# Two groups of the second layer issued by turns, pass for pass, with the product that follows them, in a fused attention and feed-forward kernel

## The chip, the cores and the metric

The kernel runs on one core of a Trainium2 chip. The metric is the device time of one execution in microseconds (us), as the median of several runs. The engines are named as in the profile: PE is the matrix engine, PEld its weight loads, DVE the vector engine, ACT the scalar engine, SP the queue that issues the DMAs.

## The reference

For each of four batches the columns of q and k are normalised over the 6080 tokens, a 256 by 256 score matrix is made and put through a softmax, v is multiplied by it, and the result goes through a feed-forward layer with an exact GELU.

```python
qn = q / (np.linalg.norm(q, axis=1, keepdims=True) + 1e-06)      # q, k, v: (4, 6080, 256)
kn = k / (np.linalg.norm(k, axis=1, keepdims=True) + 1e-06)
s = kn.transpose(0, 2, 1) @ qn / tau
a = np.exp(s - s.max(-1, keepdims=True)); a /= a.sum(-1, keepdims=True) + 1e-09
x = (v @ a).reshape(24320, 256)
h = x @ w_in                                                      # (256, 2048)
g = 0.5 * h * (1.0 + erf(h / sqrt(2)))
out = g @ w_out                                                   # (2048, 256)
```

## The kernel before

**Numbers in two parts.** Every operand of a large product is held as a rounded high part and the rest, the low part. A product of two such operands takes three matmuls into one PSUM bank: high weights by high data, low weights by high data, high weights by low data. They are called the three passes of a group here; `passes` (L649) issues them. Each pass loads its own 128 by 128 weights.

**Steps.** The attention matrix is folded into w_in for each batch (`w_part`, L557), so that the main loop (L1140) is a feed-forward layer over v. It has 4 batches b, 6 pairs p of token tiles in each batch (512 tokens a tile, 480 in the sixth pair) and 8 steps u in each pair, one for two blocks of 128 hidden units: 192 steps. From the third pair of batch 0 on, a step's first layer is seven products instead of eight, by Strassen's scheme (`first_products`, L716, in the order of `ORDER`, L647). They fill two PSUM banks by turns, `one` and `two`: product 0 goes into `one`, product 1 into `two`, product 2 is added onto `one`, product 3 onto `two`, and so on. The two banks are h0 and h1 (both stand as `h` in the profile); which of them is `one` changes from step to step through `ring` (L168 to L177). After product 0 ACT copies bank `one` to SBUF (tile `p`, from `kept`, L721), and product 2 may not touch the bank before that copy is done. After later products DVE adds a kept copy (tile `h`), and ACT makes the GELU of it: as `gh` and `g` with DVE's difference `gl` for two of the four blocks, as `x` for the other two (`whole`, L684), from which `sums` (L691) makes the sums that Strassen's second layer needs.

**The second layer** runs one step behind. `second_products` (L800) is a generator; the main loop takes one group of it after each of the products 0 to 3 of the next step, two after products 4 and 5, and the other three behind the last product (L1149 to L1157, the counts in `PLAN["units"]`). Its first four groups, made by `group` (L819), are 512 (480) columns wide and add gh and gl into the banks c10, c11, c10, c11; these are the large groups. Seven groups of half the width follow, into the banks p0, p1, c00 and c01. So PE's order in a step is product 0, large group 1, product 1, large group 2, product 2, large group 3, product 3, large group 4, product 4, and then products and small groups.

**Work that shares the banks h0 and h1.** At the end of some steps the scores of a later batch are made: `burst` (L286) issues eight matmuls into a bank that it takes from `ring`, and DVE adds that bank onto the tile `sacc`, or copies it there for the first ones of a batch (L295 to L301). In other steps `w_part` issues six matmuls into such a bank, and ACT scales it out into the tile `hl` (with `rden`, L575). Both run from `run(i, 8)`, just ahead of the next step's product 0. The bank that they take is the one that the next step's product 1 writes, because `one` of that step is the other. The steps are set by numbers in `PLAN`: `bursts` and `wpart`, counted from the start of a batch's 48 steps.

**Order.** From step 8 on the three engines' instructions keep the order in which the program issues them (`InOrder`, L179). Semaphore waits are put on the instruction that needs them.

Of the kernel before, what the change touches and what calls it, by code (L numbers as in the profile page):

```python
# [28 lines left out]
NU = NFT // 2  # L29
# [14 lines left out]
PLAN = {  # L44
    "first": {
        "splits": (10, 11, 13, 14, 15, 16, 17, 18, 19, 20, 21, 22, 24, 25, 26, 27, 28, 29, 31, 32, 33, 34),
        "loads": (8, 9, 11, 12, 13, 14, 15, 16, 17, 18, 19, 20, 22, 23, 24, 25, 26, 27, 29, 30, 31, 32),
        "bursts": ((12, 13), (14, 15), (16, 17), (18, 19), (20, 21), (22, 23), (25, 26), (27, 28), (29, 30), (32, 33), (34, 35)),
        "norms": (9, 10, 11, 12, 13, 14, 15, 16, 17, 19, 20, 21, 22, 23, 25, 26, 27, 28, 29, 30, 31, 32, 33, 34),
    },  # L50
    "later": {
        "splits": (2, 3, 5, 6, 7, 8, 10, 11, 13, 14, 16, 17, 19, 20, 21, 22, 24, 26, 27, 28, 30, 32, 33, 34),
# [35 lines left out]
    "halves": 0,  # L88
    "late": 4,
    "wat": 4,  # L90
}

EXTRAS = PLAN["extras"]
# [22 lines left out]
def channel_attention_gelu_ffn(ctx, tc, qk, kqt, vt, tau, w_in, w_out, out):  # L116
# [20 lines left out]
    ps = ctx.enter_context(tc.tile_pool(name="ps", bufs=1, space=bass.MemoryType.PSUM))  # L137

    whs = [const.tile([P, 7, 2, P], F32R, name="wh0")]
    wls = [const.tile([P, 7, 2, P], F32R, name="wl0")]  # L140
# [24 lines left out]
    def psum(name):  # L165
        return ps.tile([P, NT], F32, name=name)
# [3 lines left out]
    def bank():  # L170
        name = ring.popleft()
        ring.append(name)
        return psum(name)
# [21 lines left out]
    mm = pe.matmul  # L195
# [14 lines left out]
    def give(*tiles):  # L210
        for t in tiles:
            room.append(owner.pop(id(t))[0])
# [434 lines left out]
    ORDER = ((A11, B11), (S1, T1), (S2, T2), (S4, B22), (S3, T3), (A12, B21), (A22, T4))  # L647

    def passes(o, wh, wl, hi, lo, start, stop):  # L649
        mm(o, wh, hi, start=start, stop=False, skip_group_check=True)  # L650
        mm(o, wl, hi, start=False, stop=False, skip_group_check=True)
        mm(o, wh, lo, start=False, stop=stop, skip_group_check=True)

    def product(b, p, u, a, v, ps, start, stop):
        n = PAIRS[p][1]
        g, q = divmod(u, 2)
        hi, lo = vops[b, p, v]
        passes(ps[:, :n], whs[g][:, a, q], wls[g][:, a, q], hi[:, :n], lo[:, :n], start, stop)

    def strassen(b, p, u):  # L660
        return (b, p) > (0, 1) and (b, p, u) != (B - 1, NP - 1, NU - 1)
# [3 lines left out]
    def flush():  # L665
        for x in pending:
            x()
        pending.clear()

    def gelu(src, n, i, j):  # L670
        if j == 1:
            gh = pg.tile([P, NT], F32R, name="gh", bufs=2)
            gl = pg.tile([P, NT], F32R, name="gl", bufs=2)
        else:
            gh = pg.tile([P, 4, C] if i == 0 else [P, 3, C], F32R, name=f"gh{i}", bufs=1)
            gl = pg.tile([P, 4, C] if i == 0 else [P, 3, C], F32R, name=f"gl{i}", bufs=1)
            gh, gl = (t.rearrange("p k c -> p (k c)") for t in (gh, gl))
        g = pg.tile([P, NT], F32, name="g", bufs=2)
        act.activation(out=gh[:, :n], in_=src, func=AF.Gelu)
        act.activation(out=g[:, :n], in_=src, func=AF.Gelu)  # L680
        pending.append(lambda: dve.tensor_tensor(out=gl[:, :n], in0=g[:, :n], in1=f32(gh[:, :n]), op=ALU.subtract))
        return gh, gl
# [33 lines left out]
    def first_products(b, p, u):  # L716
# [15 lines left out]
        def do(i, ps, start, stop):  # L732
            product(b, p, u, *ORDER[i], ps, start, stop)
            if u == NU - 1:
                give(*vops.pop((b, p, ORDER[i][1])))
# [34 lines left out]
    def plain_products(b, p, u):  # L770

        n = PAIRS[p][1]
        g, q = divmod(u, 2)
        out = state["blocks"] = {}
        wh, wl = whs[g], wls[g]
        a21 = a21s[g]
        rows = {1: ((wh[:, A11, q], wl[:, A11, q]), (wh[:, A12, q], wl[:, A12, q])),
                0: ((a21[:, 0, q], a21[:, 1, q]), (wh[:, A22, q], wl[:, A22, q]))}
        cols = {0: (B11, B21), 1: (B12, B22)}
        for j in (1, 0):  # L780
            for i in (1, 0):
                ps = bank()
                for k in range(2):
                    hi, lo = vops[b, p, cols[j][k]]
                    passes(ps[:, :n], *rows[i][k], hi[:, :n], lo[:, :n], k == 0, k == 1)
                    if k == 0:
                        yield
                out[i, j] = gelu(ps[:, :n], n, i, j)
                flush()
                if u % 2 == 1 and (i, j) == (0, 0):  # L790
                    give(a21)
                if u == NU - 1 and i == 0:
                    for x in cols[j]:
                        give(*vops.pop((b, p, x)))
                if (i, j) != (0, 0):
                    yield
# [3 lines left out]
    def second_products(b, p, u, blocks):  # L800

        t0, n = PAIRS[p]
        h = n // 2
        wo = wos.pop((b, p, u))
        mine = strassen(b, p, u)
        po = pos.setdefault((b, p), {})
        mixed = any(strassen(b, p, x) for x in range(NU))

        def acc(name):
            first = name not in po  # L810
            if first:
                po[name] = psum(name)
            return po[name], first

        def wpair(c, i):
            cs = slice(c * P, (c + 1) * P)
            return wo[:, 0, i, cs], wo[:, 1, i, cs]

        def group(i, j, c):  # L819
            o, first = acc(f"c{j}{c}")  # L820
            gh, gl = blocks[i, j]
            passes(o[:, :n], *wpair(c, i), gh[:, :n], gl[:, :n], first, u == NU - 1 and i == 0)

        def evict(j, c):
            if c == 0:
                po["osb"] = pg.tile([P, NCT, NT], F32, name="osb", bufs=2)
                act.copy(out=po["osb"][:, 0, :n], in_=po[f"c{j}0"][:, :n])
            else:
                dve.tensor_copy(out=po["osb"][:, 1, :n], in_=po[f"c{j}1"][:, :n])
                store(b, p, j, po["osb"])  # L830

        for i in (1, 0):
            for c in range(NCT):
                group(i, 1, c)
                if u == NU - 1 and i == 0:
                    evict(1, c)
                yield
        if not mine:
            end = u == NU - 1
            for x in range(2 * NCT):  # L840
                c, i = divmod(x, NCT) if end and mixed else (x % NCT, x // NCT)
                i = 1 - i
                group(i, 0, c)
                if end and i == 0:
                    if mixed:
                        merge(b, p, c)
                    else:
                        evict(0, c)
                yield
            return  # L850
        ws = wss.pop((b, p, u))
        (hb, lb), (ht, lt) = blocks["b"], blocks["t"]
        last = not any(strassen(b, p, x) for x in range(u + 1, NU))
        work = (("p0", 0, wpair(0, 1), hb, lb, 0), ("p0", 1, (ws[:, 0, 1], ws[:, 1, 1]), ht, lt, 2),
                ("p1", 0, (ws[:, 0, 0], ws[:, 1, 0]), ht, lt, 0), ("p1", 1, (ws[:, 0, 2], ws[:, 1, 2]), ht, lt, 1),
                ("c00", 1, wpair(0, 0), hb, lb, 2), ("c00", 0, (ws[:, 0, 3], ws[:, 1, 3]), hb, lb, 1),
                ("c01", 1, wpair(1, 0), ht, lt, 3))
        for name, half, w, hi, lo, k in work:
            o, first = acc(name)
            passes(o[:, half * h:(half + 1) * h], *w, hi[:, k * h:(k + 1) * h], lo[:, k * h:(k + 1) * h], first, last)  # L860
            if last and name == "c01" and u < NU - 1:
                flush()
                for _ in combine(b, p):
                    pass
            yield

    def store(b, p, j, osb):

        t0, n = PAIRS[p]
        t = b * N + t0 + j * n  # L870
        dst = out[:, t:t + n].rearrange("(t p) n -> p t n", p=P)
        step = 1 if (b, p) == (B - 1, NP - 1) else NCT
        for c in range(0, NCT, step):
            nc.sync.dma_start(out=dst[:, c:c + step], in_=osb[:, c:c + step, :n])
# [265 lines left out]
    for i, (b, p, u) in enumerate(steps):  # L1140
# [7 lines left out]
        mine = strassen(b, p, u)  # L1148
# [25 lines left out]
        if mine:  # L1174
            next(rest)
        count = 11 if mine else 8
        second = second_products(b, p, u, state.pop("blocks"))
    flush()
    for _ in second:
# [30 lines left out]
```

## Time and profile before

| what | value |
|---|---|
| median of 3 runs (lowest, highest) | 2134.31 us (2133.82, 2134.33) |
| profiled execution, its own time | 2132.88 us |
| its span, first to last instruction | 2131.1 us |
| granted PE clock over the span | 1.000 |
| busy share PE, PEld, DVE, ACT | 100%, 86%, 83%, 77% |
| instructions on PE: matmuls, weight loads | 11255, 11255 |

The timeline view has one row for each instruction: its start in us from the start of the span, its length in us, the engine, the line (L188 is the helper through which all of PE's, DVE's and ACT's work goes), the operation, the tile it writes `<-` the tiles it reads, and the shape. Rows of equal instructions that follow each other are merged (x2). In brackets stands the idle time of that engine ahead of it and who ended it. Matmuls are pipelined: a matmul 512 columns wide has a length of 0.39 us, but the next one starts 0.23 us after it, so that the spacing of starts and not the length is what a matmul costs.

### The profile page before, as it was taken

The page shows a single profiled execution, that of the slowest core. Times are in us where ns is not written, and L with a number is a line of the kernel's source. Part 1 is how long each engine was busy: PE and PEld are TensorE (multiplying, and loading weights), DVE is VectorE, ACT ScalarE, POOL GpSimd, SP SyncE. Part 2 cuts the span into 40 slices and gives each one's busy share as a digit, 9 for nine tenths or more (in the row PEclk, how much of TensorE's full clock was granted, in tenths as well). Part 3 has the DMA queues.
Part 4 walks back from the last instruction along what each step waited for, and adds up shares of the span by engine and source line. Part 5 has one row for each costly group of instructions (what it writes and reads, how often), then busy time and mean ns, then how long its engine had stood idle before and what let it go on. Part 6 is the DMA issues. An engine that isn't in the chain of part 4 may idle for free.

```text
span 2131.1 us, 30717 instructions
## 1 busy us (share of the span) xinstructions
PE 2126.0 (100%) x11255; PEld 1829.4 (86%) x11255; DVE 1764.9 (83%) x2784; ACT 1640.2 (77%) x2708; POOL 1.3 (0%) x8
## 2 busy tenths in 40 slices
PE   9999999999999999999999999999999999999999
PEld 8888888888888888888888888888888888888888
DVE  7987888888888788888888888888888887787786
ACT  6867778868788788776778887877777777777776
POOL 0000000000000000000000000000000000000000
PEclk9999999999999999999999999999999999999999
DMA  9545656554356565544444655554244343343332
GB/s 384 189 162 186 226 186 201 198 183 158 140 176 208 172 204 192 195 166 143 163 159 162 209 179 192 197 196 137 110 167 166 108 151 123 116 155 121 119 133 94
DMA packets 110727, 363.76 MB, mean 171 GB/s; under 512 B 11760, under 2 KB 15984, under 8 KB 108528
## 3 DMA queue, kind: packets, MB, share of 16 engines
q1 hardware_dynamic: 110576, 361.81, 48.8%
q8 instruction: 88, 1.44, 0.3%
q14 instruction: 63, 0.52, 0.1%
HBM read 324.27 MB, written 37.49 MB: 170 GB/s over the span
## 4 chain that ended last, share of the span: by engine, by line
PE 100%; DVE 0%; ACT 0%; issue 0%; DVEq 0%; POOL 0%; POOLq 0%
PE h L188 51%; PE c L188 36%; PE p L188 13%; DVE small L188 0%; DVE t L188 0%; DVE nt L188 0%; ACT t L188 0%; ACT nt L188 0%; DVE diag L188 0%; DVE osb L188 0%; ACT rqs L188 0%; DVEq L1206 0%; ACT small L188 0%; POOL ones L152 0%; POOL ident masks.py:197 0%
## 5 line engine op out<-in xcount | busy, mean ns | idle before, releaser
L188 PE MATMUL h<-v,wh 128*128 128x512 f32 (+1 forms) x2622 | 1026.1, 391 | 0.0
L188 PE MATMUL c<-gh,wo 128*128 128x512 f32 (+3 forms) x2372 | 653.1, 357 | 0.0
L188 PEld LDWEIGHTS h<-v,wh 128*128 128x128 f32 x2622 | 493.9, 188 | 86.1 <-ACT p L188 3.9
L188 PE MATMUL h<-v,wl 128*128 128x512 f32 (+1 forms) x1311 | 513.6, 392 | 0.0
L188 PEld LDWEIGHTS c<-gh,wo 128*128 128x128 f32 x2372 | 433.0, 188 | 83.2
L188 PE MATMUL c<-gl,wo 128*128 128x512 f32 (+3 forms) x1186 | 428.5, 361 | 0.0
L188 DVE TENSOR_TENSOR gl<-x,gh 128x768 fp32r<-128x768 f32 (+1 forms) x350 | 377.0, 1077 | 48.1 <-ACT gh L188 48.0
L188 ACT ACTIVATE gh<-h 128x512 fp32r<-128x512 f32 (+1 forms) x401 | 250.8, 626 | 209.6 <-DVE h L188 195.9
L188 ACT CAST gh<-x 128x768 fp32r<-128x768 f32 (+1 forms) x350 | 327.8, 937 | 31.5 <-DVE x L188 25.1
L188 DVE TENSOR_TENSOR x<-x 128x256 f32<-128x256 f32 (+2 forms) x557 | 274.9, 496 | 57.9 <-ACT x L188 40.0
L188 DVE TENSOR_TENSOR h<-h,p 128x512 f32<-128x512 f32 (+1 forms) x368 | 251.4, 683 | 72.4 <-PE h L188 62.5
L188 DVE TENSOR_TENSOR gl<-g,gh 128x512 fp32r<-128x512 f32 (+1 forms) x418 | 284.3, 681 | 20.4 <-ACT g L188 19.4
L188 ACT COPY p<-h 128x512 f32<-128x512 f32 (+1 forms) x368 | 213.0, 579 | 112.3 <-PE h L188 112.2
L188 PEld LDWEIGHTS h<-v,wl 128*128 128x128 f32 x1311 | 246.9, 188 | 34.4
L188 PEld LDWEIGHTS c<-gl,wo 128*128 128x128 f32 x1186 | 223.6, 188 | 33.1
L188 ACT ACTIVATE g<-h 128x512 f32<-128x512 f32 (+1 forms) x401 | 245.0, 611 | 0.3 <-DVE gl L188 0.3
L188 ACT ACTIVATE x<-h 128x512 f32<-128x512 f32 (+1 forms) x350 | 201.6, 606 | 40.5 <-DVE h L188 38.0
L188 PE MATMUL p<-gh,ws 128*128 128x256 f32 (+1 forms) x1050 | 199.7, 279 | 0.0
L188 DVE TENSOR_TENSOR h<-h,u 128x512 f32<-128x512 f32 (+1 forms) x184 | 125.9, 684 | 82.8 <-PE h L188 80.3
L188 PEld LDWEIGHTS p<-gh,ws 128*128 128x128 f32 x1050 | 172.7, 189 | 15.2
L188 DVE TENSOR_TENSOR v<-v,v 128x512 fp32r<-128x512 f32 (+3 forms) x257 | 174.3, 679 | 0.0
L188 PE MATMUL p<-gl,ws 128*128 128x256 f32 (+1 forms) x525 | 147.1, 280 | 0.0
(129 smaller groups left out, 1928.1 us busy)
## 6 DMA issues: line engine op xcount, KB each, us to landing
wo<-keep_out SPq DMA_DIRECT2D x184, 512.0 KB, 4.5
ws<-keep_sum SPq DMA_DIRECT2D x175, 512.0 KB, 3.7
raw<-qk SPq DMA_DIRECT2D x96, 512.0 KB, 4.6
raw<-kqt SPq DMA_DIRECT2D x72, 512.0 KB, 4.0
v<-vt SPq DMA_DIRECT2D x80, 256.0 KB, 3.6
out<-osb SPq DMA_DIRECT2D x40, 512.0 KB, 2.8
hl<-keep_in SPq DMA_DIRECT2D x12, 1024.0 KB, 6.9
raw<-w_in SPq DMA_DIRECT2D x8, 512.0 KB, 6.7
```

The costliest lines, as they stand in the source:

```text
L188: r = op(*args, **kw)
```

## The change

In `passes` the three matmuls become three calls that are not made at once. `group` hands the calls of a large group to a queue `waiting` instead of issuing them when the group is one of the first two of a step (i is 1, c is 0 or 1), the step is a Strassen step and it is not the last of its pair (u below 7). The next calls that go through `issue` are those of the product that follows: `issue` puts out one waiting call ahead of each of its own. Everything else goes through `issue` with an empty queue and comes out as before.

```diff
     "late": 4,
     "wat": 4,
+    "weave": 2,
 }
...
     def passes(o, wh, wl, hi, lo, start, stop):
-        mm(o, wh, hi, start=start, stop=False, skip_group_check=True)
-        mm(o, wl, hi, start=False, stop=False, skip_group_check=True)
-        mm(o, wh, lo, start=False, stop=stop, skip_group_check=True)
+        return (lambda: mm(o, wh, hi, start=start, stop=False, skip_group_check=True),
+                lambda: mm(o, wl, hi, start=False, stop=False, skip_group_check=True),
+                lambda: mm(o, wh, lo, start=False, stop=stop, skip_group_check=True))
+
+    waiting = deque()
+
+    def issue(calls):
+        for x in calls:
+            if waiting:
+                waiting.popleft()()
+            x()
+        while waiting:
+            waiting.popleft()()
...
         def group(i, j, c):
             o, first = acc(f"c{j}{c}")
             gh, gl = blocks[i, j]
-            passes(o[:, :n], *wpair(c, i), gh[:, :n], gl[:, :n], first, u == NU - 1 and i == 0)
+            calls = passes(o[:, :n], *wpair(c, i), gh[:, :n], gl[:, :n], first, u == NU - 1 and i == 0)
+            if j == 1 and 2 * (1 - i) + c < PLAN["weave"] and mine and u < NU - 1:
+                waiting.extend(calls)
+            else:
+                issue(calls)
```

The three other places that call `passes` (`product`, `plain_products` and the small groups of `second_products`) call `issue(passes(...))`. The instructions of DVE, ACT, SP and GpSimd, their order and their waits are the same in both programs; on PE no matmul is added, dropped or given another address or another wait.

PE, a step that follows a burst, before: the last matmuls of the burst into bank h0 (the number behind a tile's name only counts tiles), product 0 into h1, large group 1 into c10, product 1 into h0.

```order
L188 MATMUL h0_8305<-hl_8078 128x256 x2
L188 MATMUL h0_8305<-hl_8216 128x256 x2
L188 MATMUL h1_8320<-v12_7757,wh1_487 128x512
L188 MATMUL h1_8320<-v12_7757,wl1_488 128x512
L188 MATMUL h1_8320<-v20_7832,wh1_487 128x512
L188 MATMUL c10_8197<-gh_8233,wo_8034 128x512 x2
L188 MATMUL c10_8197<-gl_8234,wo_8034 128x512
L188 MATMUL h0_8331<-v11_7778,wh1_487 128x512
L188 MATMUL h0_8331<-v11_7778,wl1_488 128x512
L188 MATMUL h0_8331<-v9_7915,wh1_487 128x512
```

The same place after:

```order
L189 MATMUL h0_8305<-hl_8078 128x256 x2
L189 MATMUL h0_8305<-hl_8213 128x256 x2
L189 MATMUL h1_8320<-v12_7757,wh1_487 128x512
L189 MATMUL h1_8320<-v12_7757,wl1_488 128x512
L189 MATMUL h1_8320<-v20_7829,wh1_487 128x512
L189 MATMUL c10_8197<-gh_8233,wo_8034 128x512
L189 MATMUL h0_8328<-v11_7778,wh1_487 128x512
L189 MATMUL c10_8197<-gh_8233,wo_8034 128x512
L189 MATMUL h0_8328<-v11_7778,wl1_488 128x512
L189 MATMUL c10_8197<-gl_8234,wo_8034 128x512
L189 MATMUL h0_8328<-v9_7915,wh1_487 128x512
```

Product 1's first pass, the first writer of bank h0 behind the burst, stands two places earlier and its second one place earlier; the group's second and third pass stand one and two places later; the last pass of product 1 stands where it stood. Large group 2 and product 2 are interleaved in the same way behind it.

PE, a step that follows a `w_part` (in a pair of 480 columns), before: the six matmuls of `w_part` into h0, product 0 into h1, large group 1, product 1 into h0.

```order
L188 MATMUL h0_6025<-hl_5690,sacc_5198 128x512 x6
L188 MATMUL h1_6034<-v0_4923,wh3_491 128x480
L188 MATMUL h1_6034<-v0_4923,wl3_492 128x480
L188 MATMUL h1_6034<-v9_5005,wh3_491 128x480
L188 MATMUL c10_5361<-gh_5957,wo_5786 128x480 x2
L188 MATMUL c10_5361<-gl_5958,wo_5786 128x480
L188 MATMUL h0_6046<-v22_4944,wh3_491 128x480
```

The same place after:

```order
L189 MATMUL h0_6025<-hl_5690,sacc_5198 128x512 x6
L189 MATMUL h1_6034<-v0_4923,wh3_491 128x480
L189 MATMUL h1_6034<-v0_4923,wl3_492 128x480
L189 MATMUL h1_6034<-v9_5002,wh3_491 128x480
L189 MATMUL c10_5361<-gh_5957,wo_5786 128x480
L189 MATMUL h0_6043<-v22_4944,wh3_491 128x480
L189 MATMUL c10_5361<-gh_5957,wo_5786 128x480
```

Here too the first pass that writes h0 stands two places earlier than before. In the whole program 308 groups and the 308 products behind them are interleaved so (2 in each of 154 steps: 22 Strassen pairs of 7 steps).

More of the change, by code (lines that the diff above doesn't have):

```diff
@@ L657, in product @@
         hi, lo = vops[b, p, v]
-        passes(ps[:, :n], whs[g][:, a, q], wls[g][:, a, q], hi[:, :n], lo[:, :n], start, stop)
+        issue(passes(ps[:, :n], whs[g][:, a, q], wls[g][:, a, q], hi[:, :n], lo[:, :n], start, stop))
     def strassen(b, p, u):
@@ L784, in plain_products @@
                     hi, lo = vops[b, p, cols[j][k]]
-                    passes(ps[:, :n], *rows[i][k], hi[:, :n], lo[:, :n], k == 0, k == 1)
+                    issue(passes(ps[:, :n], *rows[i][k], hi[:, :n], lo[:, :n], k == 0, k == 1))
                     if k == 0:
@@ L859, in second_products @@
             o, first = acc(name)
-            passes(o[:, half * h:(half + 1) * h], *w, hi[:, k * h:(k + 1) * h], lo[:, k * h:(k + 1) * h], first, last)
+            issue(passes(o[:, half * h:(half + 1) * h], *w, hi[:, k * h:(k + 1) * h], lo[:, k * h:(k + 1) * h], first, last))
             if last and name == "c01" and u < NU - 1:
```

## The prediction

> **What bounds the kernel now.** The page first: the span, the engines, the granted clock and the chain of work that ended last.
>
> ```profile
> span 2131.1 us, 30717 instructions
> PE 2126.0 (100%) x11255; PEld 1829.4 (86%) x11255; DVE 1764.9 (83%) x2784; ACT 1640.2 (77%) x2708; POOL 1.3 (0%) x8
> PEclk9999999999999999999999999999999999999999
> PE 100%; DVE 0%; ACT 0%; issue 0%; DVEq 0%; POOL 0%; POOLq 0%
> ```
>
> PE is busy from end to end at its full clock, and the chain is PE alone. So the time can change in two ways only: the spacing of PE's passes changes, or PE has to wait where it does not wait now. The other engines' instructions and their order stay, so what they take does not matter unless PE waits for it.
>
> The spacing comes from the timeline of a step with nothing beside it.
>
> ```profile
> 1732.90 0.83 ACT L188 CAST gh<-x 128x768 fp32r<-128x768 f32 x1
> 1733.62 0.62 PE L188 MATMUL c<-gh,wo 128*128 128x512 f32 x2
> 1734.31 0.39 PE L188 MATMUL h<-v,wh 128*128 128x512 f32 x1
> 1735.69 0.39 PE L188 MATMUL h<-v,wh 128*128 128x512 f32 x1
> ```
>
> From the first pass of product 1 (1734.31) to that of product 2 (1735.69) there are six passes, three of a product and three of a large group: 1.38 us, 0.23 us a pass. Product 1 starts 0.69 us, three passes, after the large group's start at 1733.62.
>
> **The price of a wait.** The trace of before has waits of this kind at other places. In the first one ACT's copy `p` releases a bank too late; in the second it comes just before the pass is due.
>
> ```profile
> 476.87 0.58 ACT L188 COPY p<-h 128x512 f32<-128x512 f32 x1
> 477.17 0.40 PE L188 MATMUL c<-gl,wo 128*128 128x512 f32 x1
> 477.50 0.19 PEld L188 LDWEIGHTS h<-v,wh 128*128 128x128 f32 x1 [0.37 <-ACT p L188]
> 477.51 0.50 PE L188 MATMUL h<-v,wh 128*128 128x512 f32 x1
> 477.85 0.40 PE L188 MATMUL h<-v,wl 128*128 128x512 f32 x1
> ...
> 1012.51 0.59 ACT L188 COPY p<-h 128x512 f32<-128x512 f32 x1
> 1012.98 0.40 PE L188 MATMUL c<-gl,wo 128*128 128x512 f32 x1
> 1013.15 0.19 PEld L188 LDWEIGHTS h<-v,wh 128*128 128x128 f32 x1 [0.21 <-ACT p L188]
> 1013.21 0.44 PE L188 MATMUL h<-v,wh 128*128 128x512 f32 x1
> 1013.49 0.39 PE L188 MATMUL h<-v,wl 128*128 128x512 f32 x1
> ```
>
> First: the copy ends at 476.87 + 0.58 = 477.45, and the weight load of the waiting pass starts 0.05 later. The wait holds the weight load, not only the matmul. The matmul starts with its weight load (477.51), and the next one comes 0.34 after it instead of 0.23: the late weights cost 0.11 more. The pass was due at 477.17 + 0.23 = 477.40, so the two passes lose 0.11 + 0.11 = 0.22. Second: release at 1013.10, weight load 0.05 later, the matmul in time at 1013.21, the next 0.28 after it: 0.05 lost. Both follow one rule: a pass loses nothing if its bank is released 0.16 us before it is due (0.05 to the weight load, 0.11 that the weights need ahead of time); otherwise loss = 0.16 - (due - release). It gives 0.16 + 0.05 = 0.21 and 0.16 - 0.11 = 0.05.
>
> **The change part by part.** It moves the first pass of product 1, and that of product 2, 2 x 0.23 = 0.46 us earlier. Last passes keep their places, so DVE and ACT get the products' results when they got them. The group's own later passes move back; nobody reads c10 and c11 before the end of a pair, so that costs nothing. What matters is who releases the bank that these first passes write.
>
> Product 1 in a plain step: the bank is released by ACT's GELU `x`, done by 1732.90 where the next instruction of ACT stands. The pass becomes due at 1734.31 - 0.46 = 1733.85, 0.95 us later. No loss.
>
> Product 1 behind a burst:
>
> ```profile
> 788.93 0.69 DVE L188 TENSOR_TENSOR sacc<-h,sacc 128x512 f32<-128x512 f32 x1
> 789.42 0.62 PE L188 MATMUL c<-gh,wo 128*128 128x512 f32 x2
> 789.62 0.59 ACT L188 COPY p<-h 128x512 f32<-128x512 f32 x1 [1.00 <-PE h L188]
> 790.11 0.39 PE L188 MATMUL h<-v,wh 128*128 128x512 f32 x1
> ...
> 248.61 0.68 DVE L188 TENSOR_TENSOR sacc<-h,sacc 128x512 f32<-128x512 f32 x1
> 249.52 0.39 PE L188 MATMUL h<-v,wh 128*128 128x512 f32 x1
> ```
>
> DVE's addition ends at 789.62. Today the pass is due at 790.11, 0.49 later. Interleaved it is due one pass after 789.42, at 789.65: 0.03 after the release instead of 0.16, so 0.13 lost. The addition starts as soon as the burst has ended, so PE's own work sets when it is done, and a pause of PE in one step does not help in the next one. There are 70 bursts (66 additions and 4 copies):
>
> ```profile
> L188 DVE TENSOR_TENSOR sacc<-h,sacc x69: 684/692/692, 201.4 to 1554.6; 128x512 f32<-128x512 f32 x66, 128x512 fp32r<-128x512 f32 x3
> L188 ACT ACTIVATE hl<-h,rden x28: 681/689/691, 56.2 to 1662.5; 128x512 f32<-128x512 f32 x28
> ```
>
> The lists of steps in the plan put 9 of the 70 ahead of a step that is not interleaved (steps 12 to 15 and 23 of the first list, 7 and 15 of the later one, used twice), which leaves 61. In two of them the addition is late (248.61 is one: release 249.29, due 249.52 - 0.46 = 249.06, loss 0.16 + 0.23 = 0.39). Sum: 59 x 0.13 = 7.7 us and 2 x 0.39 = 0.8 us.
>
> Product 1 behind a `w_part`: ACT's scaling (28 rows above, four of them in batch 0, ahead of any interleaving) releases the bank.
>
> ```profile
> 580.21 0.69 ACT L188 ACTIVATE hl<-h,rden 128x512 f32<-128x512 f32 x1 [0.61 <-PE h L188]
> 580.66 0.60 PE L188 MATMUL c<-gh,wo 128*128 128x480 f32 x2
> ...
> 600.92 0.69 ACT L188 ACTIVATE hl<-h,rden 128x512 f32<-128x512 f32 x1 [0.28 <-PE h L188]
> 601.40 0.62 PE L188 MATMUL c<-gh,wo 128*128 128x512 f32 x2
> ```
>
> In the sixth pair, with passes of 480 columns (spacing 0.21), the release is at 580.90 and the pass due at 580.87: loss 0.16 + 0.03 = 0.19. In the pair after it release 601.61, due 601.63: loss 0.14. Of the eight steps in a batch six lie in the sixth pair (40, 41, 43 to 46) and two behind it (48, 49), three times: 18 x 0.19 = 3.4 us, 6 x 0.14 = 0.8 us.
>
> Product 2 waits for ACT's copy `p`. It ends at 789.62 + 0.59 = 790.21; product 2 is due seven passes after 789.42, at 791.03: no loss. Where the softmax keeps ACT busy the copy is late:
>
> ```profile
> 486.07 0.57 ACT L188 COPY p<-h 128x512 f32<-128x512 f32 x1
> 486.78 0.41 PE L188 MATMUL h<-v,wh 128*128 128x512 f32 x1
> ```
>
> Release 486.64, due 486.78 - 0.46 = 486.32: loss 0.16 + 0.32 = 0.48, once in each of three batches: 1.4 us.
>
> Against this, waits that PE has now, later in a step with a new one, get shorter.
>
> ```profile
> PEld h L188 <- ACT p L188: 3.9, 16, 0.4
> ```
>
> At most these 3.9 us can go; only those in the three softmax steps stand close behind a new wait, and one such costs about 0.05 (the second example above). I take 0.2 us.
>
> The spacing of the interleaved passes themselves (308 x 6 = 1848) is not shown by the trace for this order. The nearest rows by shape, and a place early in the program where the scheduler mixed a product and a group (bank changes at four of six passes):
>
> ```profile
> L188 PE MATMUL h<-v,wh 128*128 128x512 f32 x2174 | 856.0, 394 | 0.0
> L188 PE MATMUL c<-gh,wo 128*128 128x512 f32 x1408 | 435.7, 391 | 0.0
> L188 PE MATMUL c<-gl,wo 128*128 128x512 f32 x704 | 280.2, 398 | 0.0
> L188 PE MATMUL h<-hl 128*128 128x512 f32 x280 | 74.9, 390 | 0.0
> ...
> 76.87 0.39 PE L188 MATMUL h<-v,wh 128*128 128x512 f32 x1
> 78.25 0.39 PE L188 MATMUL h<-v,v 128*128 128x512 f32 x1
> ```
>
> Six passes take 1.38 us there too, so I take no change. As bounds: three passes of a product at 394 and a group's at 391, 391 and 398 ns have a mean of 393.7. If all became as short as a burst's (390), it is 1848 x 3.7 ns = 6.8 us less; if all became as long as `c<-gl`, the pass ahead of a change from c to h (398), 1848 x 4.3 ns = 7.9 us more.
>
> Sum: 7.7 + 0.8 + 3.4 + 0.8 + 1.4 - 0.2 = 13.9 us. The profiled execution took 2132.88 us (1.8 around its span), which gives 2146.8. The median of before, 2134.31, lies 1.43 above that execution, so the forecast for a median is **2148.2 us**, 0.65% slower. A measurement of this kernel can tell about 0.2%, 4.3 us, from no change.
>
> **The rivals.**
>
> *Weights come in during the wait.* If a waiting pass had its weights loaded already, only real lateness would count, 0.05 - (due - release): 59 x 0.02 + 2 x 0.28 + 18 x 0.08 + 6 x 0.03 + 3 x 0.37 = 4.5 us, so 2138.8. For it: in the plain step nothing shows the weights to be short of time. Against it: the weight load at 477.50 stands behind the release, not ahead. The Trainium skill, "TensorE: Matmul & The Clock Gate", section "Step-by-step: what each phase is for", says that PE pulls weight loads ahead of the matmul in flight; taken as holding across a semaphore wait, that is this rival, and the row at 477.50 speaks against it. Chance 0.07.
>
> *Not slower: alternation shortens the passes.* PE would gain if a pass that does not follow another into the same bank, with the same data, were spaced more tightly. The place is the 1848 passes. To end within 0.2% it needs (13.9 - 4.3) / 1848 = 5.2 ns a pass, to end faster 9.8 ns. At 8 ns, the whole step from `c<-gl` (398) to `h<-hl` (390), it gives 14.8 us less, 2133.4. Against it: the six mixed passes at 76.87 save nothing, and `h<-hl`, the shortest, is the one that does not change banks. Chance 0.07, 0.04 of it faster.
>
> *Alternation lengthens them.* With 398 for all: 2148.2 + 7.9 = 2156.1. For it: in the large group the pass ahead of a bank change is the longest. Against: 76.87 again. Chance 0.07.
>
> *The clock drops.* If the short new gaps made the clock fall to half in the interleaved stretches, 1848 x 0.23 = 425 us would be added, 2573. Against it: PEclk is 9 in every slice although the waits at 477 and 1013 are there. The Trainium skill, same page, section "A second HAM failure mode: psum-queue depth-cycling", tells of a kernel that cycled PSUM banks in each iteration and lost its clock so; no run here shows it. Chance 0.01.
>
> **How the numbers follow.** The forecast's own case has 0.78. The range 2141.4 to 2156.1 reaches from the shortest spacing (2148.2 - 6.8) to the longest; it leaves out the first two rivals and the clock, 0.15, and some 0.03 of the forecast's own case. Slower by over 0.2% means above 2138.6: the forecast, the lengthening, the clock and half of the first rival, 0.90. Faster is 0.04, the rest, 0.06, is no change.
>
> **What would show it.** In the profile after: in the list of waits, PEld h behind DVE sacc some 61 times and behind ACT hl 24 times, which have no such rows now; at a burst, a weight load of product 1 that starts 0.05 after DVE's addition, its matmul with it, and a next pass 0.34 later; nothing new at the plain steps; six interleaved passes in 1.38 us. PE's mean lengths by shape should move by no more than 4 ns. It is wrong if interleaved passes without a wait take more or less than 0.23 each, if the weight load stands ahead of the release, or if the span grows by less than 9 us with those waits there.

## The result: 0.8% slower

| | before | after |
|---|---|---|
| median us (lowest, highest) | 2134.07 (2133.77, 2134.33) | 2151.41 (2150.63, 2151.61) |
| profiled execution us | 2132.88 | 2150.63 |
| span us | 2131.1 | 2148.8 |

The medians are of four executions each; that of before is over the three given ahead of the prediction and one more. The ratio after to before is 1.0083, with a 95% interval from 1.0071 to 1.0095. The forecast was 2148.2 with a range of 2141.4 to 2156.1.

The page of after, with its span, engines, clock and chain:

```profile
span 2148.8 us, 30717 instructions
PE 2142.9 (100%) x11255; PEld 1822.2 (85%) x11255; DVE 1765.4 (82%) x2784; ACT 1646.6 (77%) x2708; POOL 1.3 (0%) x8
PEclk9999999999999999999999999999999999999999
PE 99%; ACT 1%; DVE 1%; issue 0%; DVEq 0%; POOL 0%; ACTq 0%; POOLq 0%
```

The same matmuls at the same clock take 17.7 us more, and ACT and DVE now have a share of the chain. On this page alone the kernel still looks bound by PE and nothing else: a matmul's length hides most of a short pause, as the waiting ones below show (0.50 us long instead of 0.39). The pauses stand in the list of waits of after (engine, tile and line waited for: us in total, times, longest):

```profile
PEld h L189 <- DVE sacc L189: 18.7, 61, 0.6
PEld h L189 <- ACT hl L189: 7.5, 24, 0.3
PEld h L189 <- ACT p L189: 3.0, 6, 0.6
...
PE h L189 <- ACT p L189: 0.6, 3, 0.2
```

The first two have no counterpart in before, and they come in the numbers forecast, 61 and 24. Their microseconds are idle time of the weight loads, which without a wait run up to 0.23 us ahead of their matmul, so they are not the loss. What a wait costs is read from the timeline of after, at a softmax step, a `w_part` in the sixth pair, one in the pair behind it, a burst, and a plain step:

```profile
489.16 0.57 ACT L189 COPY p<-h 128x512 f32<-128x512 f32 x1
489.19 0.39 PE L189 MATMUL c<-gh,wo 128*128 128x512 f32 x1
489.78 0.19 PEld L189 LDWEIGHTS h<-v,wh 128*128 128x128 f32 x1 [0.63 <-ACT p L189]
489.78 0.50 PE L189 MATMUL h<-v,wh 128*128 128x512 f32 x1 [0.20 <-ACT p L189]
490.12 0.39 PE L189 MATMUL c<-gh,wo 128*128 128x512 f32 x1
...
584.65 0.69 ACT L189 ACTIVATE hl<-h,rden 128x512 f32<-128x512 f32 x1 [0.61 <-PE h L189]
585.10 0.38 PE L189 MATMUL c<-gh,wo 128*128 128x480 f32 x1
585.39 0.19 PEld L189 LDWEIGHTS h<-v,wh 128*128 128x128 f32 x1 [0.32 <-ACT hl L189]
585.71 0.38 PE L189 MATMUL c<-gh,wo 128*128 128x480 f32 x1
...
605.58 0.69 ACT L189 ACTIVATE hl<-h,rden 128x512 f32<-128x512 f32 x1 [0.28 <-PE h L189]
606.06 0.40 PE L189 MATMUL c<-gh,wo 128*128 128x512 f32 x1
606.31 0.19 PEld L189 LDWEIGHTS h<-v,wh 128*128 128x128 f32 x1 [0.29 <-ACT hl L189]
606.65 0.40 PE L189 MATMUL c<-gh,wo 128*128 128x512 f32 x1
...
795.42 0.69 DVE L189 TENSOR_TENSOR sacc<-h,sacc 128x512 f32<-128x512 f32 x1 [0.18 <-PE h L189]
795.91 0.40 PE L189 MATMUL c<-gh,wo 128*128 128x512 f32 x1
796.17 0.19 PEld L189 LDWEIGHTS h<-v,wh 128*128 128x128 f32 x1 [0.30 <-DVE sacc L189]
796.17 0.50 PE L189 MATMUL h<-v,wh 128*128 128x512 f32 x1
796.51 0.40 PE L189 MATMUL c<-gh,wo 128*128 128x512 f32 x1
...
1749.83 0.84 ACT L189 CAST gh<-x 128x768 fp32r<-128x768 f32 x1
1750.56 0.39 PE L189 MATMUL c<-gh,wo 128*128 128x512 f32 x1
1750.79 0.40 PE L189 MATMUL h<-v,wh 128*128 128x512 f32 x1
1751.95 0.39 PE L189 MATMUL c<-gh,wo 128*128 128x512 f32 x1
```

At the burst DVE's addition ends at 796.11 and the weight load starts at 796.17, its matmul with it. The pass was due at 795.91 + 0.23 = 796.14, and the next one starts 0.34 behind it instead of 0.23: 0.03 + 0.11 = 0.14 lost. The idle time in the bracket, 0.30, is twice that. At the two `w_part` steps and at the softmax the load likewise starts 0.04 to 0.05 behind the end of ACT's instruction, and the next pass comes 0.32 to 0.34 later. At all 85 waits of the first two rows the load starts 0.050 to 0.054 us behind the release, and its matmul 1 to 2 ns behind the load.

Which instruction waits can be read from the instruction records of the trace: 2393 of PE's 11255 weight loads carry a semaphore wait, and none of its 11255 matmuls does, in before as in after. The sentence on the kernel's order, that a wait is put on the instruction that needs it, means for PE the weight load ahead of the matmul. So it is the program as it ran that makes the weights wait for the bank, although only the matmul writes it.

In the plain step nothing waits; six passes take 1750.56 to 1751.95, 1.39 us.

The mean lengths by shape in after:

```profile
L189 PE MATMUL h<-v,wh 128*128 128x512 f32 x2174 | 863.6, 397 | 0.8 <-ACT p L189 0.6
L189 PE MATMUL c<-gh,wo 128*128 128x512 f32 x1408 | 479.8, 393 | 0.0
L189 PE MATMUL c<-gl,wo 128*128 128x512 f32 x704 | 278.9, 396 | 0.0
L189 PE MATMUL h<-hl 128*128 128x512 f32 x280 | 74.9, 389 | 0.0
```

None moved by more than 3 ns from 394, 391, 398 and 390, and the 3 of the first row hold the pauses. Lengths are therefore of no use here; starts are.

Every matmul of after can be set beside the same place in before, and the starts compared unrounded. PE's last matmul starts 17.72 us later. Of these, 17.18 arise inside the 308 interleaved blocks (six passes each, to the start of the next pass) and 0.55 everywhere else:

| released by | blocks | ns more per block | us | forecast us |
|---|---|---|---|---|
| DVE's addition, burst | 55 | 147 | 8.11 | 7.7, both |
| DVE's copy, burst | 4 | 151 | 0.60 | |
| DVE's late additions | 2 | 392 | 0.78 | 0.8 |
| ACT's scaling, sixth pair / behind it | 18 / 6 | 187 / 137 | 3.36 + 0.82 | 3.4 + 0.8 |
| softmax, copy `p` | 3 | 437 | 1.31 | 1.4 |
| product 1 without a wait, 512 wide | 59 | 15.0 | 0.88 | 0 |
| product 2 without a wait, 512 wide | 123 | 6.7 | 0.82 | 0 |
| without a wait, 480 wide, product 1 / product 2 | 10 / 28 | 6.8 / 14.6 | 0.07 + 0.41 | 0 |

### The profile page after: what moved, and what is told of

It is laid out like the page before. It is cut to its first block, busy times and chain, and to the rows that moved or that the text cites. A ratio compares the mean times of both kernels' runs of the same rounds, so it can differ in the third digit from the quotient of the medians.

```text
span 2148.8 us, 30717 instructions
## 1 busy us (share of the span) xinstructions
PE 2142.9 (100%) x11255; PEld 1822.2 (85%) x11255; DVE 1765.4 (82%) x2784; ACT 1646.6 (77%) x2708; POOL 1.3 (0%) x8
## 4 chain that ended last, share of the span: by engine, by line
PE 99%; ACT 1%; DVE 1%; issue 0%; DVEq 0%; POOL 0%; ACTq 0%; POOLq 0%
PE h L189 51%; PE c L189 35%; PE p L189 13%; ACT L189 0%; ACT gh L189 0%; DVE gl L189 0%; DVE x L189 0%; DVE osb L189 0%; ACT p L189 0%; DVE small L189 0%; DVE h L189 0%; DVE sacc L189 0%; DVE t L189 0%; ACT x L189 0%; DVE nt L189 0%
## 5 line engine op out<-in xcount | busy, mean ns | idle before, releaser
L189 PE MATMUL c<-gh,wo 128*128 128x512 f32 (+3 forms) x2372 | 706.4, 358 | 0.0
L189 PEld LDWEIGHTS h<-v,wh 128*128 128x128 f32 x2622 | 493.4, 188 | 112.3 <-DVE sacc L189 18.7
```

What stands on the lines that cost most here:

```text
L189: r = op(*args, **kw)
```

## The experiments

*Late release*, the theory on record: apart from the spacing of its passes, a block loses time only where the bank of its first pass is released less than 0.16 us before that pass is due. The rival, *alternation itself*: each of the 308 blocks costs 17.3 / 308 = 0.056 us for being issued by turns. The times below stand beside 2133.17 us for before in the first four runs, 2133.20 in the other four. The expectations of the first four were added to 2134.07, so the increments are what to compare.

**One group alone, either way.** Only large group 1 by turns with product 1:

```diff
-            if j == 1 and 2 * (1 - i) + c < PLAN["weave"] and mine and u < NU - 1:
+            if j == 1 and i == 1 and c == 0 and mine and u < NU - 1:
```

> Only large group 1 runs by turns with product 1; group 2 stands whole ahead of product 2 as before. Theory of the late release: product 1's first pass keeps its waits behind 61 bursts and 24 w_part steps, which the replay by the rule loss = 0.16 - (due - release) puts at 12.8 us; with about 1 us of spacing in the quiet steps some +14 us, 2148, and PEld h waiting for DVE sacc 61 times and for ACT hl 24 times as in the changed kernel. Rival, alternation itself costs 17.3 us / 308 groups = 0.056 us a group wherever it stands: 154 groups, +8.7 us, 2142.8.

Only large group 2 with product 2 (`c == 1` in the same line):

> Only large group 2 runs by turns with product 2. Theory of the late release: of these 154 places only the three in the softmax steps have a late copy, 1.4 us, and 1.2 us of spacing: about +2.5 us, 2136.6, with no wait of PEld h for DVE sacc or ACT hl. Rival, alternation itself costs: again 154 groups, +8.7 us, 2142.8.

Measured 2149.44 us (ratio 1.0076, 1.0062 to 1.0090) and 2136.94 (1.0017, 1.0008 to 1.0027). The rival wants both halves alike; the first costs 16.3, the second 3.8. Late release had +14 and +2.5, and both came out higher. The interleaved blocks of the second show 2.1 us of spacing for the 1.2 taken. In the first another 1.8 us stand outside the interleaved blocks, in large group 2 and product 2: these are issued whole as in before, but lose 13.3 ns in each of the 123 plain blocks of 512 columns. The list of waits of the first:

```profile
PEld h L189 <- DVE sacc L189: 18.7, 61, 0.5
PEld h L189 <- ACT hl L189: 7.4, 24, 0.3
```

These are the rows of after, with group 1 alone. The second kernel has neither row.

**The quiet blocks alone.** The groups ahead of a late release are issued as before: group 1 in the steps behind a burst or a `w_part`, group 2 in the softmax steps. The other 219 of the 308 stay by turns.

```diff
-            if j == 1 and 2 * (1 - i) + c < PLAN["weave"] and mine and u < NU - 1:
+            if (j == 1 and 2 * (1 - i) + c < PLAN["weave"] and mine and u < NU - 1
+                    and not late_release((b * NP + p) * NU + u, c)):
```

> Both groups run by turns, but not group 1 of a step behind a burst or a w_part, nor group 2 of the softmax steps: 219 of the 308 groups are left, all at places where the bank has been released in time. Theory of the late release: no wait is left, only the spacing of the passes: 0 to +2.2 us, 2134.1 to 2136.3. Rival, alternation itself costs: 219 x 0.056 = +12.3 us, 2146.4.

Measured 2136.16 us, ratio 1.0014 (1.0005 to 1.0022): 3.0 us for 219 blocks, where the rival wants 12.3 and late release 0 to 2.2. Inside the 219 blocks the starts show 2.44 us more; 0.69 lies outside them. So most of the loss is in the blocks left out. Of these 89, 88 have a late release; the other is group 2 of the same step in the last batch, where no softmax runs.

**One pass later.** All 308 groups by turns, but the product starts one pass later, c c h c h h:

```diff
     def issue(calls):
+        if waiting:
+            waiting.popleft()()
         for x in calls:
```

> All 308 groups run by turns, but the product starts one pass later: group, group, product, group, product, product. A first pass of a product stands one place (0.23 us) earlier than before instead of two. Theory of the late release: behind a burst the release is then 0.25 us ahead of the due time and behind a w_part 0.21 or 0.25, more than 0.16, so nothing is lost there; what is left is 0.3 us at the two late additions and 0.8 us at the three softmax copies, so +1 to +3 us, 2135.2 to 2137.3. Rival, alternation itself costs: four bank changes in a block where before there were two and in the changed kernel six, half the price, +8.7 us, 2142.8. If the wait cost only its lateness, not the weights too, this kernel would come out the same as under the first theory but the changed one would not have lost 0.13 us a burst.

Measured 2135.55 us, ratio 1.0011 (1.0002 to 1.0020). The timeline at the same burst:

```profile
790.38 0.69 DVE L189 TENSOR_TENSOR sacc<-h,sacc 128x512 f32<-128x512 f32 x1
790.87 0.62 PE L189 MATMUL c<-gh,wo 128*128 128x512 f32 x2
791.12 0.19 PEld L189 LDWEIGHTS h<-v,wh 128*128 128x128 f32 x1
791.32 0.39 PE L189 MATMUL h<-v,wh 128*128 128x512 f32 x1
```

The weight load still starts 0.05 behind the addition (791.07), but now it is 0.20 ahead of its matmul, more than the 0.11 it needs: nothing is lost. Only the two late additions still cost 0.30 us. One place in PE's order, 0.23 us, is the difference between 17.3 us and 2.4.

**One pass earlier.** The product leads, h c h c h c:

```diff
         for x in calls:
+            x()
             if waiting:
                 waiting.popleft()()
-            x()
```

> Kernel after with the product's pass ahead of the group's in each pair of passes (h c h c h c instead of c h c h c h): its first pass stands three places, 0.69 us, ahead of its place in the kernel before, instead of two. Late release (loss = 0.16 us - (due - release), from the trace of before, now with another 0.23 us of lateness where there was some): behind bursts 21.3 us of DVE's additions and 1.5 of copies, behind w_part 9.3, softmax copies 2.6, sum 34.7, and the spacing of some +2 that the kernel after showed: 2133.2 + 36.7 = 2169.9 us. In the trace a pause behind DVE's additions at a burst of about 0.36 us each. Rival, weights come in during the wait (only real lateness costs): about 0.11 us less at each of the 87 places, 2160 us. Rival, the alternation itself costs 0.056 us a group wherever it stands: as the kernel after, 2150.5.

Measured 2170.65 us (2169.80 to 2171.14), ratio 1.0174 (1.0160 to 1.0188), 37.5 us more than before against 36.7 by the rule; weights coming in during the wait would have given 2160, alternation itself 2150.5. The list of waits and the timeline at the same burst:

```profile
PEld h L189 <- DVE sacc L189: 32.7, 61, 0.8
PEld h L189 <- ACT hl L189: 12.7, 24, 0.5
```

```profile
791.20 0.69 DVE L189 TENSOR_TENSOR sacc<-h,sacc 128x512 f32<-128x512 f32 x1 [0.46 <-PE h L189]
791.45 0.99 PE L189 MATMUL h<-v,wh 128*128 128x512 f32 x2
...
791.94 0.19 PEld L189 LDWEIGHTS h<-v,wh 128*128 128x128 f32 x1 [0.53 <-DVE sacc L189]
...
792.29 0.39 PE L189 MATMUL c<-gh,wo 128*128 128x512 f32 x1
```

The row with x2 holds product 0's last pass (791.45) and product 1's first, due at 791.68. The addition ends at 791.89, 0.21 behind that. The pass starts with its weight load at 791.94 and the next one 0.35 later: 0.26 + 0.12 = 0.38, where the rule gives 0.16 + 0.21 = 0.37. The number of waits is the same as in after, 61 and 24; each is one pass longer. Behind all 61 bursts the starts show 23.1 us more (22.8 by the rule), behind the 24 `w_part` steps 9.5 (9.3). So the price grows with the lateness and keeps its constant part.

**The release earlier.** Bursts and `w_part` run three small groups earlier, first in the kernel before and then in the one after:

```diff
-    "burst": 8,
-    "part": 8,
+    "burst": 7,
+    "part": 7,
```

> Kernel before with bursts and w_part three groups earlier in their step (slot 7 for 8 in both entries of the plan): the control for the next kernel. Both theories: the same passes, none by turns, so 2133.2 within 4 us either way; a loss, if there is one, is of a burst's own start, which may find its input or its bank less ready 1.06 us earlier.

> Kernel after with bursts and w_part three groups earlier (slot 7 for 8), by turns as before. Late release: DVE's addition or ACT's scaling ends about 1.06 us earlier against the first pass of product 1, so the waits behind DVE's additions (8.9 us), the copies at bursts (0.6) and w_part (4.2) all go, and against the kernel with slot 7 alone only the softmax copies (1.3) and the spacing (some 2.2) stay: 3.5 us more than that one, about 2136.7 us if slot 7 itself is free. In the list of waits, the weight loads behind DVE sacc and ACT hl disappear. Rival, the alternation itself costs 0.056 us a group wherever it stands: 17.3 us more than the one with slot 7 alone, about 2150.5.

Measured 2147.38 us for the first (ratio 1.0066, 1.0052 to 1.0080), and 2151.99 for the second (1.0088, 1.0074 to 1.0102). The difference is 4.6 us, 3.5 by late release, 17.3 by the rival. The two profiled executions are 4.9 us apart, and the 308 blocks hold 4.5 us of that: 1.3 in the softmax steps as forecast, and 3.1 of spacing where 2.2 was taken, because the blocks that no longer wait also lose by being issued by turns, 14.9 ns behind each of the 61 bursts and 11.9 (480 wide) or 8.8 (512) behind a `w_part`. The second kernel at the burst:

```profile
788.53 0.69 DVE L189 TENSOR_TENSOR sacc<-h,sacc 128x512 f32<-128x512 f32 x1 [1.08 <-PE h L189]
...
790.06 0.39 PE L189 MATMUL c<-gh,wo 128*128 128x512 f32 x1
...
790.29 0.40 PE L189 MATMUL h<-v,wh 128*128 128x512 f32 x1
```

The addition ends at 789.22, 1.07 us before product 1 is due, and the rows behind DVE sacc and ACT hl are gone from the list of waits although the groups are issued by turns.

The control itself missed by 14 us. Its list of waits and its timeline at the burst say why:

```profile
PEld h L188 <- DVE h L188: 18.0, 52, 0.9
PEld h L188 <- ACT g L188: 5.5, 4, 1.4
```

```profile
784.66 0.68 DVE L188 TENSOR_TENSOR h<-h,p 128x512 f32<-128x512 f32 x1
785.40 1.46 PEld L188 LDWEIGHTS h<-hl 128*128 128x128 f32 x8 [0.22 <-DVE h L188]
785.45 1.61 PE L188 MATMUL h<-hl 128*128 128x512 f32 x8
```

The burst takes its bank from an addition of DVE that belongs to the step's last products, and that ends at 785.34; the burst's weight load starts 0.06 later. Moved ahead of three groups, the burst overtakes its own release. Of the gaps between starts that exceed the usual one by over 25 ns, those at the starts of bursts and `w_part` sum to 8.5 us in this kernel, and those at the first two passes of a product, four of them behind ACT's `g`, to 7.3 where before has 1.9. Together that is 13.9 of the 14.75 us by which the spans of the two profiled executions differ; the starts in the first 50 us, ahead of every burst and `w_part`, already differ by 0.85, for a reason not looked into. So the control lost mostly by the same kind of wait at other places.

**One group, one pass later.** Group 1 alone, c c h c h h:

```diff
     def issue(calls):
+        if waiting:
+            waiting.popleft()()
         for x in calls:
...
-            if j == 1 and 2 * (1 - i) + c < PLAN["weave"] and mine and u < NU - 1:
+            if j == 1 and i == 1 and c == 0 and mine and u < NU - 1:
```

> Only group 1 by turns with product 1, and product 1 one pass later than in the kernel after (c c h c h h): its first pass 0.23 us ahead of its place in the kernel before. Late release, replayed on the trace of before: 0.3 us of waits; spacing as the kernel with that order for both groups showed in block 1 (7 ns less in six passes, 154 blocks): 1.0 us less. Sum 2133.2 - 0.7 = 2132.5, which a measurement can't tell from before. Rival, the alternation itself costs 0.056 us a group: 2133.2 + 8.6 = 2141.8.

Measured 2134.72 us (2133.73 to 2135.08), ratio 1.0006 (0.9997 to 1.0015): no difference that can be told, so no order tried here beats the kernel before. Its 154 blocks sum to +0.25 us, the shorter spacing (7 ns in each of 59 plain blocks) being given back by the two late additions (0.32 us) and by longer gaps at the other blocks. Large group 2 and product 2, issued whole behind them, take 0.74 us more, and 0.96 lies elsewhere and is not traced to a place; so the 1.0 us less that the expectation took for spacing did not come.

## Why the prediction was right, and what it mis-sized

**The bound and the path.** PE sets the time, and the change costs mostly where PE newly waits. This is shown by the quiet blocks (3.0 us for 219) and by the rows of the kernel with group 1 alone.

**The rule, loss = 0.16 - (due - release).** It was taken from two waits of before and held in 88 blocks, at the burst, the scaling and the softmax, and again with each of the waits 0.23 us later: 37.5 us against 36.7. In each of the 85 blocks behind a burst or a `w_part` the loss measured in after is within 17 ns of the rule's, the spacing included. The constant part is real: had the weights come in during the wait, the forecast's first rival, after would have lost 4.5 us by its waits.

The forecast's reason against that rival does not hold, though. It took the row at 477.50 as evidence that PE does not load weights ahead across a semaphore wait. As the records show, the wait stands in the weight load itself, so the load could not have gone ahead, and no run here has a wait on a matmul alone. Whether the 0.11 us would vanish if the wait stood on the matmul was not tried. That the 0.11 us is the time of late weights is an inference from the starts: load and matmul start together, and the next pass comes 0.11 us late.

**The terms of the sum.** Bursts 8.71 us for 7.7, late additions 0.78 for 0.8, `w_part` 4.18 for 4.2, softmax 1.31 for 1.4. The measured ones include the spacing of their blocks, which the forecast had at nothing; without it the waits are 13.8 us for 14.1. The bursts' 147 ns are the rule's 0.13 plus the 15 ns that a plain block of product 1 loses as well: 147 - 15 = 132. The kernel by turns with the earlier release shows that 15 at the same bursts, without a wait.

**The spacing, taken as no change, is the term that was mis-sized.** The six mixed passes at 76.87 were taken to show that it costs nothing. Without a wait the blocks lost 15.0 ns (product 1), 6.7 (product 2) and on average 12.5 (480 wide), 2.18 us together; with an estimated 1.15 us of the same kind inside the 88 blocks that wait (67 of product 1 with 512 columns by 15.0, 18 with 480 by 6.8, three of the softmax by 6.7) it is 3.3 us. The bounds held it (-6.8 to +7.9). Rows rounded to 0.01 us could hardly show 15 ns in 1.38 us, and the mixed passes at 76.87 were in another order (h c h h c c) than that of the change; the order of the passes matters to a few nanoseconds, as below. Neither of the rivals on spacing is what happened: alternation did not shorten the passes, and it lengthened them by less than half of the 7.9 us.

**Waits that shrink.** 0.2 us was to come back outside the blocks; it came out at +0.55. The waits of ACT's copies in the softmax steps did shrink (0.19 us in each of three), 0.57 together where 0.2 was forecast, and small gaps elsewhere grew by more. Outside the blocks the kernels with group 2 alone and with the quiet blocks come to 0.4 and 0.7 us, so these gaps are not resolved by one execution.

The sum of the steps as measured, 13.8 us of waits, 3.3 of spacing and 0.55 of the rest, is the 17.7 us between the two profiled executions; 13.9 was forecast. The forecast for the median is closer, 2148.2 for 2151.41, partly by luck: it added 1.43 us because the median of before lay that far above its profiled execution, and in after this came to 0.78. The clock stayed at 1.000, so the last rival falls too.

## What to carry to other kernels

Before an instruction of the saturated engine is moved earlier, look up in the trace when the buffer that it writes is released, in each kind of step and not only in the plain one, and charge the price of a wait as the trace of before shows it. Here 15.0 of the 17.7 us sit in 88 of 308 blocks, and one place in the order decides between 2.4 and 17.3 us. Look up, too, on which instruction the wait stands: here it holds the weight load as well as the matmul, and a release that comes before the matmul is due can still be late. Idle time in a list of waits isn't the loss: the weight loads' 18.7 us behind DVE's additions stood for 8.6 (the first three rows of the table less 61 times 15 ns), and the engine's busy share stayed at 100%.

## What the runs showed of the hardware that was not expected

The spacing of passes without any wait depends on their order, and on that of the passes ahead of them. Six passes of large group and product in the plain steps late in the program, from start to start, unrounded means in ns:

```
kernel                      block 1               block 2
before                      c c c h h h  1378.3   c c c h h h  1380.0
after                       c h c h c h  1393.5   c h c h c h  1386.5
group 1 alone               c h c h c h  1393.4   c c c h h h  1384.9
group 2 alone               c c c h h h  1378.3   c h c h c h  1395.0
one pass later              c c h c h h  1371.4   c c h c h h  1386.9
one group, one pass later   c c h c h h  1371.7   c c c h h h  1386.7
```

Single gaps run from 225 to 237 ns and repeat from step to step within 1 or 2 ns. They do not follow the number of bank changes: c c h c h h changes banks more often than c c c h h h, and in block 1 it is 6.9 ns shorter. Nor does a block's own order decide alone: behind a changed block 1, block 2 takes 1384.9 to 1386.9 in all three orders, also whole as in before. With the product one pass later block 2 gives back what block 1 gains, and the two together take the 2758.3 ns of before. By turns, one block alone costs 15.0 (group 2) or 19.9 ns (group 1) in the two blocks together, both 21.7. What sets a gap was not tried and stays open.
